# Whether GpSimd or ScalarE makes the upper halves of the first 14 pieces of weights

## The chip, the cores and the metric

One core of a Trainium2 chip runs the whole program. The metric is device time in microseconds (us) from start to end of one launch. The engines are named as the profile names them: PE is TensorE (PEld its weight loads), ACT is ScalarE, DVE is VectorE, POOL is GpSimd and SP the SyncE queue that issues DMAs.

## The reference

Attention with a cut just under each row's maximum, then two feed-forward layers on its output. The attention works on 4 batches of 8 heads with 576 rows of 64 numbers.

```python
scores = scale * q @ k.T                       # per batch and head, 576 x 576
thresh = max(scores, axis=-1) - tau
scores = where(scores >= thresh, scores, -1e9)
attn = exp(scores - max(scores)); attn /= sum(attn) + 1e-09
x = (attn @ v), heads side by side              # 2304 x 512
g = x @ w_gate                                  # d_ff 1536
x = (silu(g) * (x @ w_val)) @ w_out
h = maximum(x @ w_in, 0)                        # d_ff 2048
out = (h * h) @ w_out2                          # 2304 x 512
```

The weights come as float64. The kernel reads their 64-bit words and rebuilds float32 numbers from the bits on the chip, then splits each into a high part that the PE's fast float32 form holds exactly and a low rest, so that three fast products stand for one exact product.

## The kernel before

**Attention.** The work is 144 tiles of 128 rows by 576 columns, nine for each pair of heads and 36 for each batch. Every tile takes the same path. `QK` on the PE makes the scores `s` (two PSUM banks in turn, `s_115` and `s_116` in the orders below). `RED` on DVE takes the row maximum. `CUT` on ACT writes `z`, of which there is one buffer. `EXP` on ACT writes `e` (three buffers, `e_104` to `e_106`) and the row's sum. `RCP` on DVE makes `r`. `NORM` on POOL (line 684) multiplies `e` by `r`. `TR` on the PE transposes `e` into PSUM (five products against `ident`, line 706). `PH` on DVE or ACT copies the transposes to `x_65` (called `x`), and for four of nine tiles `AV` on the PE multiplies by the values (line 762). `QK` of the next tiles runs ahead of `TR`: the tile that is transposed is two or three behind.

**Weights beside it.** While the attention of the first batch runs, the class `Loader` brings in the first 30 pieces of weights, each 128x256 numbers. A piece passes through five steps, written as a generator that yields the engine of its next step. SP loads the 64-bit words (`xF<-in_w`, line 143) into one of three buffers. `few_steps` then copies the top 16 bits of each word into the upper half of a 32-bit word of `head` as a float16 (line 173; two buffers, `head_81` and `head_82`). DVE ors in the middle bits, which gives the float32 piece (line 175, output `xF` or `wf`). ACT copies it to its high part (`wa` or `wx`, line 68), and POOL subtracts to get the low part (`wa<-..,wa`, line 76).

**What sets the order.** In the loop over tiles, `loader.tick(engine)` writes at most one next step of the pieces that wait for that engine, at fixed places of the iteration. A list scheduler then places the instructions with the offsets of the tables `early0` and `early` (`LP` is the tick of POOL, `LA` of ACT, `LD` of DVE). Each engine runs its own list strictly in that order. From tile 36 on, the first feed-forward layer for the finished batch is worked into the attention of the next ones (line 256 is its first product), and after the attention the remaining layers run on the PE alone.

Of the kernel before, what the change touches and what calls it, by code (L numbers as in the profile page):

```python
# [17 lines left out]
AF = mybir.ActivationFunctionType  # L18
# [4 lines left out]
P = 128  # L23
# [59 lines left out]
def attention_moe(tc, qkv, qk0, tau, w1, w2, out, cfg):  # L83
    nc = tc.nc
    ops = Ops(nc)
# [33 lines left out]
    class Loader:  # L119
# [48 lines left out]
        def few_steps(self, raw, fl, whi, wlo, n):  # L168

            head = self.heads[n % len(self.heads)]  # L170
            upper = head.bitcast(F16).rearrange("p (n two) -> p n two", two=2)[:, :, 1]
            yield "A"
            nc.scalar.activation(upper, raw.top, AF.Copy)
            yield "D"
            nc.vector.scalar_tensor_tensor(
                fl.bitcast(I32), raw.mid, 13, head.bitcast(I32), op0=ALU.logical_shift_right, op1=ALU.bitwise_or
            )
            yield "A"
            ops.copy("A", whi, fl)
            yield cfg["wl"][0]  # L180
            ops.sub(cfg["wl"][0], wlo, fl, whi.bitcast(F32))
# [21 lines left out]
    loader = Loader()  # L203
# [253 lines left out]
    heads = {}  # L457
# [388 lines left out]
    def work(i):  # L846

        fstate["credit"] += cfg["rate"]
        if avq:
            at_(AV, avq.pop(0))  # L850
            if fstate["credit"] < cfg["extra"]:
                return
        if fstate["credit"] > 0:
            y = at_(fill_group)
            if y is None:
                fstate["credit"] = 0
            else:
                fstate["credit"] -= y
# [12 lines left out]
    def at_(f, *args, name=None):  # L871
        if name in ("LD", "LA") and 8 <= fstate["i"] < 16:

            with tc.issue_after(st[1]["red" if name == "LD" else "exp"]):
                return f(*args)
        off = cfg["early0" if fstate["i"] < 9 * NPAIR else "early"].get(name or f.__name__, 0)
        if not off:
            return f(*args)
        with tc.high_priority(offset=off):
            return f(*args)  # L880

    for i in range(NTILE + lag + 1):
        mp1.age += 1
        fstate["i"] = i
        t = i - lag - 1
        if i == cfg["three"] + lag:
            mp1.banks = deque(bank[2:])
        if i >= cfg["ldat"] and (i % cfg["lev"] == 0 or i >= 9 * NPAIR):
            at_(loader.start, name="LS")
        at_(loader.tick, "D", name="LD")  # L890
        if i < NTILE:
            at_(RED, i)
            at_(CUT, i)
        if 0 <= t < NTILE:
            at_(PH, t)
            at_(NEG, t)
        if i < NTILE:
            at_(EXP, i)
        at_(loader.tick, "D", name="LD")
        at_(loader.tick, "A", name="LA")  # L900
        at_(mp1.flush, "D", name="FD")
        if 0 <= t < NTILE:
            at_(PL, t)
            if tiles[t][2] in PARTS:
                avq.append(t)
        if 0 <= i - 1 < NTILE:
            at_(RCP, i - 1)
            at_(NORM, i - 1)
        at_(loader.tick, "D", name="LD")
        at_(mp1.flush, "A", name="FA")  # L910
        if i + 1 < NTILE:
            at_(QK, i + 1)
        work(i)
        if 0 <= i - lag < NTILE:
            at_(TR, i - lag)
        at_(mp1.flush, "P", name="FP")
        at_(loader.tick, "P", name="LP")
        at_(loader.tick, "A", name="LA")
        if i < NTILE:
            b, p, k = tiles[i]  # L920
            ha = b * H + 2 * p
            pr = i // 9
            if pr == 0:
                for _ in range((0, 1, 2)[k] if k < 3 else 0):
                    next(first)()
            elif k < 2:
                at_(next, steps, name="PS")
            if pr + 1 < B * NPAIR and k >= 2:
                if k == 2:
                    steps = pair_steps(pr + 1)  # L930
                at_(next, steps, name="PS")
        at_(loader.tick, "D", name="LD")
# [652 lines left out]
def pack(inputs):  # L1585
# [51 lines left out]
    "zs": 1,  # L1637
    "wl": "PD",
    "live": (3, 2),
    "fill": 6,  # L1640
    "om": "D",
    "early0": {
# [19 lines left out]
def program(arrays):  # L1662
    import concourse.bacc as bacc

    nc = bacc.Bacc("TRN2", target_bir_lowering=False, num_devices=1, dynamic_dma_scratch_size=512)
    args = [nc.dram_tensor(n, a.shape, mybir.dt.from_np(a.dtype), kind="ExternalInput").ap() for n, a in arrays]
    out = nc.dram_tensor("out_0_dram", (NT, DM), F32, kind="ExternalOutput").ap()
    with tile.TileContext(nc) as tc:
        attention_moe(tc, *args, out, CFG)
    return nc  # L1670
# [9 lines left out]
```

## Time and profile before

| | |
|---|---|
| median of three runs | 1140.37 us (1140.35 to 1140.4) |
| the profiled execution, whole | 1141.48 us |
| its span, first to last instruction | 1139.7 us |
| busy in the span: PE, DVE, ACT, POOL | 1110.3, 847.6, 678.5, 241.2 us |
| granted clock of the PE | 0.998 |

Busy time is the time in which an engine runs an instruction. An engine that waits for another shows as idle, and the profile names what ended the wait. Ends of the PE's products are modelled, so a busy PE can still hold short waits. 1.8 us of the profiled execution lie outside its span.

### The profile page before, as it was taken

The page shows a single profiled execution, that of the slowest core. Times are in us where ns is not written, and L with a number is a line of the kernel's source. Part 1 is how long each engine was busy: PE and PEld are TensorE (multiplying, and loading weights), DVE is VectorE, ACT ScalarE, POOL GpSimd, SP SyncE. Part 2 cuts the span into 40 slices and gives each one's busy share as a digit, 9 for nine tenths or more (in the row PEclk, how much of TensorE's full clock was granted, in tenths as well). Part 3 has the DMA queues.
Part 4 walks back from the last instruction along what each step waited for, and adds up shares of the span by engine and source line. Part 5 has one row for each costly group of instructions (what it writes and reads, how often), then busy time and mean ns, then how long its engine had stood idle before and what let it go on. Part 6 is the DMA issues. An engine that isn't in the chain of part 4 may idle for free.

```text
span 1139.7 us, 19554 instructions
## 1 busy us (share of the span) xinstructions
PE 1110.3 (97%) x6572; PEld 1010.2 (89%) x6572; DVE 847.6 (74%) x2088; ACT 678.5 (60%) x1594; POOL 241.2 (21%) x365
## 2 busy tenths in 40 slices
PE   7988999999999999999999999989999999999998
PEld 6777999899999999998888888889898998899997
DVE  7887887877787864889985888687658677866554
ACT  7888888988888873554432444345556455543221
POOL 6667655545464521000000000000000000000000
PEclk9999999999999999999999999999999999999999
DMA  7766433344343300332210234355355445443542
GB/s 211 221 190 178 105 96 96 98 110 110 91 100 96 96 1 28 93 93 84 84 56 11 72 141 152 108 175 195 144 207 176 176 158 194 153 159 123 193 174 77
DMA packets 55827, 143.15 MB, mean 126 GB/s; under 512 B 7600, under 2 KB 8880, under 8 KB 55728
## 3 DMA queue, kind: packets, MB, share of 16 engines
q1 hardware_dynamic: 55584, 141.92, 40.4%
q8 instruction: 52, 0.85, 0.3%
q14 instruction: 47, 0.39, 0.1%
q10 hardware_dynamic: 144, 0.00, 0.0%
HBM read 93.06 MB, written 22.28 MB: 101 GB/s over the span
## 4 chain that ended last, share of the span: by engine, by line
PE 79%; DVE 6%; ACT 4%; DMA 2%; issue 1%; POOL 0%; POOLq 0%; ACTq 0%; DVEq 0%; SPq 0%
PE mm L256 17%; PE mm L1490 17%; PE mm L1437 13%; PE mm L301 8%; PE bank L256 6%; PE s L648 4%; PE bank L706 4%; PE bank L765 4%; PE bank L301 4%; DMA wr<-in_w_dram 2%; ACT z L666 1%; DVE st__108 L658 1%; ACT e L674 1%; DVE xs_m L76 1%; ACT pt L726 1%
## 5 line engine op out<-in xcount | busy, mean ns | idle before, releaser
L706 PE MATMUL bank<-ident,e 128*128 128x128 f32 (+1 forms) x720 | 150.5, 275 | 9.3 <-ACT x L68 3.3
L684 POOL TENSOR_SCALAR e<-e,r 128x576 f32<-128x576 f32 x144 | 112.7, 783 | 132.5 <-DVE r L679 106.5
L76 DVE TENSOR_TENSOR pt<-bank,pt 128x384 fp32r<-128x384 f32 x216 | 100.5, 486 | 51.2 <-ACT pt L726 49.5
L256 PE MATMUL mm<-xs,wa 128*128 128x512 f32 (+2 forms) x672 | 125.7, 347 | 0.5 <-ACT x L68 0.5
L256 PEld LDWEIGHTS mm<-xs,wa 128*128 128x128 f32 x672 | 109.5, 188 | 15.7 <-ACT x L68 0.7
L666 ACT ACTIVATE z<-s,thr 128x576 f32<-128x576 f32 x144 | 106.7, 741 | 27.3 <-DVE st__108 L658 21.0
L658 DVE TENSOR_SCALAR_CACHE_REDUCE st__108<-s,tau_c 128x576 bf16<-128x576 f32 x144 | 116.9, 812 | 5.1 <-PE s L648 3.3
L256 PE MATMUL bank<-xs_m,wa 128*128 128x288 f32 x576 | 108.5, 321 | 2.5 <-DVE xF L777 0.9
L706 PEld LDWEIGHTS bank<-ident,e 128*128 128x128 f32 (+1 forms) x720 | 91.2, 135 | 17.3 <-issue 4.6
L674 ACT ACTIVATE e<-z 128x577 f32<-128x577 f32 x144 | 99.5, 691 | 1.7
L726 ACT ACTIVATE pt<-bank 128x384 fp32r<-128x384 f32 x216 | 88.4, 437 | 18.6 <-PE bank L706 17.1
L256 PEld LDWEIGHTS bank<-xs_m,wa 128*128 128x128 f32 x576 | 87.0, 188 | 5.5 <-DVE xs_m L76 2.0
L765 PE MATMUL bank<-pt,vs 128*128 128x256 f32 (+1 forms) x480 | 90.5, 318 | 0.4 <-ACT pt L726 0.3
L648 PE MATMUL s<-kh,qs 128*128 128x288 f32 x256 | 77.9, 318 | 7.6 <-DVE qs L534 5.9
L256 PE MATMUL mm<-xs,wb 128*128 128x512 f32 (+1 forms) x360 | 74.9, 368 | 0.0
L1507 DVE TENSOR_TENSOR xF<-xF,mm 128x512 f32<-128x512 f32 x54 | 37.0, 685 | 50.9 <-PE mm L1490 50.9
L765 PEld LDWEIGHTS bank<-pt,vs 128*128 128x128 f32 x480 | 71.9, 189 | 1.6 <-ACT pt L726 0.7
L648 PE MATMUL s<-kl,qs 128*128 128x288 f32 x256 | 73.1, 300 | 0.0
L256 PEld LDWEIGHTS mm<-xs,wb 128*128 128x128 f32 x360 | 62.9, 189 | 11.3
L68 ACT ACTIVATE wb<-wf 128x256 fp32r<-128x256 f32 x82 | 34.0, 414 | 65.2 <-DVE wf L1094 39.6
L1091 ACT ACTIVATE wf<-wr 128x256 f32<-128x256 f32 x64 | 27.6, 433 | 73.5 <-DMA wr<-in_w_dram 55.1
L1490 PE MATMUL mm<-wb,wx 128*128 128x512 f32 x270 | 67.1, 389 | 0.0
(154 smaller groups left out, 2550.8 us busy)
## 6 DMA issues: line engine op xcount, KB each, us to landing
wr<-in_w_dram SPq DMA_DIRECT2D x106, 256.0 KB, 2.9
raw<-in_qkv_dram SPq DMA_DIRECT2D x15, 896.0 KB, 4.6
kh<-land SPq DMA_DIRECT2D x60, 144.0 KB, 2.6
kl<-raw SPq DMA_DIRECT2D x60, 144.0 KB, 2.8
xF<-in_w_dram SPq DMA_DIRECT2D x30, 256.0 KB, 3.4
right<-kept1T SPq DMA_DIRECT2D x8, 768.0 KB, 5.3
right<-kept0T SPq DMA_DIRECT2D x7, 768.0 KB, 5.4
right<-kept SPq DMA_DIRECT2D x6, 768.0 KB, 4.4
```

Of the source, the lines that this page charges most:

```text
L76: e.tensor_tensor(out, a, b, op=ALU.subtract)
L256: mm(pt[:, :n], w[:, a, col + c * P : col + (c + 1) * P], xs[:, b, c, :], start=(i == 0), stop=(i == len(TERMS) - 1),)
L301: mm(pt[:, :n], w[:, a, 2 * DM + m * P : 2 * DM + (m + 1) * P], u[:, b, :], start=(k == 0), stop=(k == last),)
L648: mm(sp[:, cols], l, r[:, cols], start=(n_ == 0), stop=(n_ == len(pairs) - 1),)
L658: red = nc.vector.tensor_scalar(st_, st[t]["s"][:, :S], scalar1=tau_c, scalar2=None, op0=ALU.subtract, op1=ALU.max, accum_out=th)
L666: nc.scalar.activation(z[:, :S], st[t]["s"][:, :S], AF.Prelu, bias=st[t]["thr"], scale=-1.0, alpha=1 / SLOPE)
L674: ex = nc.scalar.activation(e, st[t]["z"], AF.Exp, scale=-SLOPE, accum_out=sum_)
L684: nc.gpsimd.tensor_scalar(e, e, scalar1=r, scalar2=1.0, op0=ALU.mult, op1=ALU.mult)
L706: mm(dst[:n, j], e[:, c0 : c0 + n], ident, is_transpose=True, start=(j == 0), stop=(j == 1),)
L765: mm(o[:, :n], hd["vs"][:, SLOT[k % 5], :], pt[:, k, lo : lo + n], start=(k == 0), stop=(k == 9))
L1437: mm(bank[:, :BK], w[:, a, c * P : (c + 1) * P], t[:, b, c, :], start=(n == 0 and x in ("11", "12", "S1")), stop=(n == 5), skip_group_chec ...
L1490: mm(pt, u[:, b, s * P : (s + 1) * P], w[a], start=(half == 0 and j == 0 and i == 0), stop=(half == 1 and j == 1 and i == 2),)
```

## The change

The generator's first step for a piece now yields POOL for pieces 1 to 14 and ACT for the rest, and the copy goes through the helper that POOL's other copies use (a multiplication by 1 twice, line 72 in the profile). POOL's tick stands twice in an iteration, so that two of its steps can be written there.

```diff
@@ -169,8 +169,9 @@
             head = self.heads[n % len(self.heads)]
             upper = head.bitcast(F16).rearrange("p (n two) -> p n two", two=2)[:, :, 1]
-            yield "A"
-            nc.scalar.activation(upper, raw.top, AF.Copy)
+            eng = "P" if n <= cfg["heads"] else "A"
+            yield eng
+            ops.copy(eng, upper, raw.top)
             yield "D"
@@ -914,7 +915,8 @@
         at_(mp1.flush, "P", name="FP")
-        at_(loader.tick, "P", name="LP")
+        for _ in range(2):
+            at_(loader.tick, "P", name="LP")
         at_(loader.tick, "A", name="LA")
@@ -1637,6 +1639,7 @@
     "live": (3, 2),
+    "heads": 14,
     "fill": 6,
```

Behind the first changed line, line numbers are one higher in the new kernel (two from the tick on, three behind the table's new row). The new order differs at three places that matter.

POOL at its first work on scores, before. `qt` are two small copies for tile 4, `e_104`, `e_105` and `e_106` the `NORM` of tiles 0, 1 and 2, `kl_187` the low part of the second head's keys.

```order
L548 TENSOR_SCALAR qs_185<-raw_182,qscale 128x576
L72 TENSOR_SCALAR qt_124<-qs_144 128x64
L72 TENSOR_SCALAR qt_125<-qs_185 128x64
L684 TENSOR_SCALAR e_104<-e_104,r_175 128x576
L76 TENSOR_TENSOR kl_187<-raw_182,kh_186 128x288 x2
L684 TENSOR_SCALAR e_105<-e_105,r_196 128x576
L684 TENSOR_SCALAR e_106<-e_106,r_222 128x576
L76 TENSOR_TENSOR raw_212<-raw_212,land_214 128x288 x2
L684 TENSOR_SCALAR e_104<-e_104,r_246 128x576
```

POOL at the same place now:

```order
L549 TENSOR_SCALAR qs_185<-raw_182,qscale 128x576
L72 TENSOR_SCALAR head_82<-xF 128x256
L72 TENSOR_SCALAR head_81<-xF 128x256
L72 TENSOR_SCALAR qt_124<-qs_144 128x64
L72 TENSOR_SCALAR qt_125<-qs_185 128x64
L685 TENSOR_SCALAR e_104<-e_104,r_175 128x576
L72 TENSOR_SCALAR head_82<-xF 128x256
L685 TENSOR_SCALAR e_105<-e_105,r_196 128x576
L76 TENSOR_TENSOR kl_187<-raw_182,kh_186 128x288 x2
L76 TENSOR_TENSOR wa<-xF,wa 128x256
L72 TENSOR_SCALAR head_81<-xF 128x256
L685 TENSOR_SCALAR e_106<-e_106,r_222 128x576
```

Two heads now stand ahead of the two `qt` and the `NORM` of tile 0, a third ahead of that of tile 1. `kl_187` has moved behind the `NORM` of tile 1.

PE from the last two transposes of tile 0 (`bank_89<-ident,e_104`) on, before. The products into `s_115` are the first four of eight of `QK` of tile 4.

```order
L706 MATMUL bank_89<-ident,e_104 128x128 x2
L648 MATMUL s_115<-kh_145,qt_124 128x288
L648 MATMUL s_115<-kl_146,qt_124 128x288
L648 MATMUL s_115<-kh_186,qt_125 128x288
L648 MATMUL s_115<-kl_187,qt_125 128x288
```

PE at the same place now:

```order
L707 MATMUL bank_89<-ident,e_104 128x128 x2
L707 MATMUL bank_90<-ident,e_105 128x128
L707 MATMUL bank_90<-ident,e_105 64x128
L707 MATMUL bank_90<-ident,e_105 128x128
L649 MATMUL s_115<-kh_145,qt_124 128x288
L649 MATMUL s_115<-kl_146,qt_124 128x288
L649 MATMUL s_115<-kh_186,qt_125 128x288
L649 MATMUL s_115<-kl_187,qt_125 128x288
```

The first three transposes of tile 1 (`e_105`) stood behind all eight products of tile 4 and now stand ahead of them.

ACT from `CUT` of tile 4 (`thr_239`) to `EXP` of tile 6, before:

```order
L666 ACTIVATE z_107<-s_115,thr_239 128x576
L68 ACTIVATE x_65<-bank_90 128x2x128
L674 ACTIVATE e_105,sum_244<-z_107 128x577
L173 ACTIVATE head_81<-xF 128x256
L666 ACTIVATE z_107<-s_116,thr_264 128x576
L68 ACTIVATE wa<-xF 128x256
L674 ACTIVATE e_106,sum_269<-z_107 128x577
L68 ACTIVATE wa<-wf_80 128x256
L666 ACTIVATE z_107<-s_115,thr_285 128x576
L68 ACTIVATE x_65<-bank_88 128x2x128
L674 ACTIVATE e_104,sum_290<-z_107 128x577
```

ACT at the same place now:

```order
L667 ACTIVATE z_107<-s_115,thr_239 128x576
L68 ACTIVATE x_65<-bank_90 128x2x128
L675 ACTIVATE e_105,sum_244<-z_107 128x577
L68 ACTIVATE wa<-wf_80 128x256
L667 ACTIVATE z_107<-s_116,thr_264 128x576
L68 ACTIVATE wa<-xF 128x256
L675 ACTIVATE e_106,sum_269<-z_107 128x577
L68 ACTIVATE wa<-xF 128x256
L667 ACTIVATE z_107<-s_115,thr_285 128x576
L68 ACTIVATE x_65<-bank_88 128x2x128
L675 ACTIVATE e_104,sum_290<-z_107 128x577
```

The head between `EXP` of tile 4 and `CUT` of tile 5 is gone, and copies of the high part (`wa`) take such places earlier. Over `CUT` of tiles 0 to 17 the list of ACT holds 12 heads and 11 high parts before, and no head and 14 high parts now. From tile 19 on it holds heads at the same tiles as before (19, 19, 21, 21, 23, 26 and so on), of pieces two later, and the last two heads, at tile 41, are gone. DVE's list follows: the first two combinations stand ahead of `RED` of tile 3, which also moves behind the two copies of tile 0's transposes; over tiles 0 to 17 DVE has 14 combinations (11 before) and POOL 14 subtractions (11 before). On the PE the order is the same from tile 13 to the end but for some single transposes.

## Rows read from the trace of the kernel before

**Rows 1.** Busy time, instructions, clock and DMA of stretches.

```profile
core 0: us, PE busy (x) PEld busy (x) DVE busy (x) ACT busy (x) POOL busy (x), PEclk, DMA share, GB/s
...
10.00:50.00 40.00, 38.01 (x219) 32.10 (x219) 33.95 (x94) 36.86 (x90) 27.08 (x38) 1.00 0.71 200
50.00:98.00 48.00, 42.14 (x249) 34.80 (x248) 38.23 (x106) 41.24 (x100) 32.12 (x44) 1.00 0.72 196
...
120.00:1139.00 1019.00, 1006.29 (x5956) 921.57 (x5954) 752.13 (x1827) 575.92 (x1348) 163.83 (x244) 1.00 0.38 118
```

**Rows 2.** What the PE waited for, 10 to 60 us (total, times, longest).

```profile
PE bank L706 <- POOL e L684: 1.3, 2, 1.1
PE s L648 <- ACT z L666: 0.5, 2, 0.3
PE bank L762 <- DVE x L70: 0.2, 1, 0.2
```

**Rows 3.** The same, from 60 us on.

```profile
PE bank L706 <- ACT x L68: 3.3, 5, 1.1
```

**Rows 4.** Groups of ACT, 10 to 50 us: busy us, mean ns | idle before.

```profile
L173 ACT ACTIVATE head<-xF 128x256 f16<-128x256 bf16 x12 | 5.8, 495 | 0.0
...
L68 ACT ACTIVATE wa<-xF 128x256 fp32r<-128x256 f32 x7 | 2.9, 419 | 0.0
```

**Rows 5.** Groups of DVE, 10 to 50 us.

```profile
L175 DVE SCALAR_TENSOR_TENSOR xF<-xF,head 128x256 int32<-128x256 int32 x7 | 3.7, 547 | 0.0
...
L175 DVE SCALAR_TENSOR_TENSOR wf<-xF,head 128x256 int32<-128x256 int32 x4 | 2.5, 627 | 0.3 <-ACT head L173 0.3
```

**Rows 6.** Groups of POOL, 10 to 50 us.

```profile
L684 POOL TENSOR_SCALAR e<-e,r 128x576 f32<-128x576 f32 x17 | 13.7, 808 | 7.9 <-DVE r L679 6.9 <-PE bank L762 0.5 <-PE bank L706 0.4
L76 POOL TENSOR_TENSOR wa<-xF,wa 128x256 fp32r<-128x256 f32 x7 | 5.1, 732 | 0.2 <-ACT wa L68 0.2
L76 POOL TENSOR_TENSOR raw<-raw,land 128x288 fp32r<-128x288 f32 x4 | 3.7, 929 | 2.3 <-ACT land L68 2.3
...
L72 POOL TENSOR_SCALAR qt<-qs 128x64 fp32r<-128x64 f32 x5 | 1.4, 280 | 2.3 <-DVE qs L534 1.7 <-DMA qs<-raw 0.6
```

**Rows 7.** The tile head over the span: ns min/median/max.

```profile
L175 DVE SCALAR_TENSOR_TENSOR xF<-xF,head x20: 394/426/933, 13.6 to 116.8; 128x256 int32<-128x256 int32 x20
```

**Rows 8.** The tile xF, 0 to 13 us.

```profile
L143 SPq DMA_DIRECT2D xF<-in_w_dram x3: 327/432/646, 4.5 to 6.6; - x3
...
DMA to landing us min/median/max: 4.8/5.1/5.3
```

**Rows 9.** POOL in order of time, 5 to 13 us: start, us.

```profile
7.35 0.75 POOL L548 TENSOR_SCALAR qs<-raw,qscale 128x576 fp32r<-128x576 f32 x1 [3.12 <-DMA raw<-in_qk_dram]
...
9.97 0.24 POOL L72 TENSOR_SCALAR qt<-qs 128x64 fp32r<-128x64 f32 x1 [1.66 <-DVE qs L534]
10.19 0.75 POOL L684 TENSOR_SCALAR e<-e,r 128x576 f32<-128x576 f32 x1
11.96 1.56 POOL L76 TENSOR_TENSOR kl<-raw,kh 128x288 fp32r<-128x288 f32 x2 [1.02 <-ACT kh L68]
```

**Rows 10.** The PE in order of time, 8 to 16 us.

```profile
11.67 1.27 PE L706 MATMUL bank<-ident,e 128*128 128x128 f32 x5
12.59 0.59 PE L648 MATMUL s<-kh,qt 128*128 128x288 f32 x1
...
14.65 1.39 PE L706 MATMUL bank<-ident,e 128*128 128x128 f32 x8
15.79 0.38 PE L648 MATMUL s<-kh,qs 128*128 128x288 f32 x1
```

**Rows 11.** DVE in order of time, 8 to 20 us.

```profile
11.99 0.82 DVE L658 TENSOR_SCALAR_CACHE_REDUCE st__108<-s,tau_c 128x576 bf16<-128x576 f32 x1 [0.89 <-ACT kh L68]
```

**Rows 12.** Two stretches at the start, columns as in Rows 1.

```profile
10.00:15.00 5.00, 4.69 (x20) 4.33 (x20) 3.62 (x11) 4.83 (x11) 3.54 (x6) 1.00 0.54 217
15.00:20.00 5.00, 5.00 (x34) 4.57 (x33) 4.57 (x12) 4.50 (x13) 4.16 (x5) 1.00 0.70 184
```

## Prediction

> **What bounds the kernel now.** I began with the busy time of stretches [rows 1]. From 120 us on the PE is busy 1006.29 of 1019 us, so there every microsecond by which the attention of the first batch ends earlier is passed on, and nothing else of this change counts. The pieces 1 to 14 lie in the stretch from 10 to 50 us. There ACT is busy 36.86 of 40 us, DVE 33.95, POOL 27.08, and the PE 38.01. ACT looks like the bound by its share against DVE and POOL, but the PE is busier still. So the second view was the list of what the PE waited for: from 10 to 60 us three kinds of wait of together 2.0 us (1.3 for `NORM` on POOL, 0.5 for `CUT` on ACT, 0.2 for a copy on DVE) [rows 2]. That fits 40 less 38.01. The reader is to see that the PE runs its list nearly without a gap in the stretch in which the change takes work from ACT. The longer waits, such as 3.3 us for copies on ACT, come after 60 us [rows 3], where ACT keeps its heads.
>
> **What is taken from ACT.** Over tiles 0 to 17 ACT loses 12 heads of 0.495 us, 5.9 us, and gains three more copies of the high part of 0.419 us, because the pieces come along sooner [rows 4]: 36.86 - 5.9 + 1.3 = 32.2 us. This could shorten the stretch by 4.7 us if ACT alone set its pace. What the PE can give back is less: its waits, 2.0 us at most. Of these I count the two for `CUT` (0.5) and the one for the copy (0.2) whole, since a head less in ACT's queue brings both `CUT` and the sum for `r` sooner. Of the 1.3 us for `NORM`, 1.1 are one wait [rows 2]; the low parts of the keys (`raw<-raw,land`), which can stand ahead of a `NORM` on POOL, waited 2.3 us in all for ACT's copy `land` [rows 6]. A freer ACT makes that copy sooner, but not before its data have landed, so I take 0.9 of the 1.3. Together **1.6 us are given back**; the ends are 0 and 2.0.
>
> **What POOL pays.** The trace has no copy on POOL from 16-bit words to 16-bit words. The nearest rows are a one-input copy of 64 elements at 0.280 us and a one-input multiplication of 576 at 0.808 [rows 6]. On the line between them 256 elements take 0.280 + 192 x (0.808 - 0.280) / 512 = 0.48 us. From below I bound it by 0.28, since four times the elements of that copy cost no less, and from above by 0.93, the mean of the dearest subtraction with two inputs (288 elements). I take 0.48, because this operation has one input like the two rows on the line. Fourteen heads are 6.7 us, three more subtractions of 0.732 us are 2.2 us, and POOL comes to 27.08 + 6.7 + 2.2 = 36.0 of 40 us. It hides these in the time in which it waited for `r` before a `NORM`, 6.9 us in the stretch [rows 6]. The cover is thin: at 0.77 us for a head POOL would be full (27.08 + 2.2 + 14 x 0.77 = 40).
>
> **What the moved order costs at the start.** This is the term that is on the path for sure if the pieces land late. POOL's list now has two heads ahead of the `NORM` of tile 0. The loads of pieces 1 to 3 were issued from 4.5 to 6.6 us and took 4.8 to 5.3 us [rows 8]: the first is there at about 9.6 us, the second at about 10.6. POOL, free from 8.1 us, therefore stands still, makes the heads until 11.1, then the two `qt` (0.28 each), and starts the `NORM` at 11.65 instead of 10.19 [rows 9]. It ends at 12.4; the transposes of tile 0 on the PE, which began at 11.67, begin 0.75 us later. They took 0.92 us, until 12.59 [rows 10], so now until 13.3. A third head and the `NORM` of tile 1 end at 12.4 + 0.48 + 0.75 = 13.65. For that the PE waits, since three transposes of tile 1 now stand ahead of `QK` of tile 4; with 0.14 us each (1.14 us for eight, 14.65 to 15.79) that product starts at 14.05 instead of 12.59, and ends at 16.1 after its 2.06 us. The low keys `kl` behind that `NORM` are ready at 13.65 + 1.56 = 15.2, just before the last product needs them. Five transposes are left, 0.7 us, so the PE reaches the next `QK` at 16.8 instead of 15.79 [rows 10]. **The start loses 1.0 us.** On DVE the same shows: `RED` of tile 3, at 11.99 us before [rows 11], now stands behind two copies that need tile 0's transposes, some 2 us later; ACT had other work in between. The loss is 0 if the scheduler's places are filled by waits that POOL had anyway. From above: the PE ran 20 instructions in 4.69 busy us from 10 to 15 us and 34 in 5.00 us from 15 to 20, with the granted clock at 1.00 (2.4 GHz) in both rows [rows 12]. If its quicker pace came 3 us later because it stood idle here, 3 x (1 - 20/34) = 1.2 us more are lost, 2.2 in all.
>
> **What is free.** From tile 19 on the heads that ACT keeps stand at the same tiles, and the PE's order is the same, so from 50 to 98 us (PE 42.14 of 48 busy [rows 1]) I count no gain: that stretch only starts sooner or later as a whole. The two heads fewer at tile 41 fall where the PE is full. The loads come a little earlier and take no more queue time. DVE's three more combinations in the stretch are 3 x 0.56 = 1.7 us (6.2 us for eleven [rows 5]), 35.6 of 40, off the path while the PE is the fuller one.
>
> **The sum.** 1.0 - 1.6 = -0.6 us. For a profiled execution that is 1141.48 - 0.6 = 1140.9 us; the median of the runs shown lies 1.1 us below the profiled execution, so **1139.8 us** for the median. With the ends above the likeliest case goes from -2.0 to +2.2 us, 1138.4 to 1142.6. All of it is within 0.2% (2.3 us), about what a measurement of this kernel can tell from no change.
>
> **Rival 1, faster: ACT was the pace after all.** Ends of products are modelled, PEld is busy only 32.10 of 40 us [rows 1], and so a PE that looks full can hide small stalls behind a late `CUT`. Then the whole 4.7 us come back, less the 1.0 us of the start: -3.7, **1136.7 us**. For it speaks that the removed heads stand directly between `CUT` and `EXP` in ACT's list; against it that only 0.5 us of the PE's waits name ACT. Chance 0.25.
>
> **Rival 2, slower: POOL becomes the bound.** If the copy between 16-bit words costs 0.93 us instead of 0.48, POOL needs 27.08 + 13.0 + 2.2 = 42.3 us in 40, and `NORM`, which stands behind heads in its list, is late in every tile: +2.3. At the start the three heads are 0.9 us longer, 1.9 in place of 1.0. Together +4.2, **1144.6 us**. It decides from 0.77 us a head. Nothing in the trace shows such a price for one input. Chance 0.10.
>
> **Rival 3, slower: DVE and POOL block each other.** The combination on DVE reads two tiles in SBUF and takes 0.394 us at the least and 0.933 at the most [rows 7]; in the stretch its mean is 0.547 and 0.627 [rows 5], while POOL works 68% of the time. With POOL at 36.0 of 40, in proportion, the wait above 0.394 grows from 0.18 to 0.24 us, 14 x 0.06 = 0.8 us of DVE, which is free. If instead each of 14 combinations waited out a whole subtraction of 0.732, DVE would need 33.95 - 6.2 + 14 x 1.126 = 43.5 us in 40: +3.5, with the start's 1.0 +4.5, **1144.9 us**. Chance 0.08. The Trainium skill (SBUF — State Buffer, Who interferes with whom) has such a rule: a DVE instruction with two SBUF inputs and a GpSimd instruction that reads SBUF share a port, and the second to start waits for all of the first. By that rule work on POOL is never free to DVE, and the change moves work to the one engine that can slow DVE; the spread of 0.394 to 0.933 us agrees with it, but the means show that most combinations meet little.
>
> **How the numbers follow.** The likeliest case has 0.57, the rivals 0.25, 0.10 and 0.08. Faster by over 0.2% is rival 1, 0.25; within 0.2% the likeliest case, 0.57; slower rivals 2 and 3, 0.18. The range takes in the likeliest case's ends and rival 1, 1136.6 to 1142.6, and leaves 0.18 out.
>
> **What would show it.** Right: heads on POOL at a mean near 0.48 us; from 10 to 50 us ACT near 32, POOL near 36; the first `NORM` at about 11.65 us and `QK` of tile 4 at about 14; waits of the PE from 18 to 60 us well under 2.0 us in all; and from tile 19 on the same gaps at the same tiles, all moved by under 2 us. Wrong: a head above 0.77 us, `NORM` waited for by the PE in most tiles, or tiles 5 to 17 that follow each other clearly faster, so that the gaps of the second half come 3 us or more earlier.

## The result, and the profile after

The changed kernel takes 1146.07 us (median of 6 runs, 1143.58 to 1149.03), the kernel before beside it 1140.38 (1139.53 to 1141.28). The ratio is 1.0052, with a 95% interval of 1.0036 to 1.0067. It is slower by 5.7 us where 0.6 less were forecast. The profiled execution took 1146.45 us with a span of 1144.7, which is 5.0 more than that of before.

The first view is again the busy time of stretches (columns as in [rows 1]), here of the changed kernel.

```profile
10.00:50.00 40.00, 34.37 (x196) 28.48 (x195) 33.38 (x86) 31.31 (x72) 31.52 (x50) 1.00 0.69 197
...
120.00:1139.00 1019.00, 1010.06 (x5982) 925.51 (x5981) 753.96 (x1834) 579.08 (x1355) 164.90 (x246) 1.00 0.37 117
```

From 10 to 50 us ACT fell from 36.86 to 31.31 us and POOL rose from 27.08 to 31.52, as meant. But the PE fell from 38.01 to 34.37, with 196 instructions where there were 219. What it waited for from 10 to 60 us answers to [rows 2]:

```profile
PE bank L707 <- POOL e L685: 4.3, 5, 1.2
PE bank L763 <- DVE x L70: 0.8, 1, 0.8
PE bank L707 <- ACT x L68: 0.4, 1, 0.4
PE s L649 <- ACT z L667: 0.3, 1, 0.3
PE bank L707 <- DVE x L70: 0.2, 1, 0.2
```

2.0 us of waits have become 6.0, and 4.3 of them are for `NORM` on POOL (line 685 now). From 60 us on little changed (3.1 us for ACT's copies, 3.3 in [rows 3]). The PE in order of time shows four of the five places, 3.9 us: one where tile 0 is transposed, and three more in tiles 3 to 5.

```profile
12.63 2.05 PE L707 MATMUL bank<-ident,e 128*128 128x128 f32 x8 [0.81 <-POOL e L685]
14.32 0.59 PE L649 MATMUL s<-kh,qt 128*128 128x288 f32 x1
...
17.62 0.38 PE L649 MATMUL s<-kh,qs 128*128 128x288 f32 x1
...
21.39 0.76 PE L707 MATMUL bank<-ident,e 128*128 128x128 f32 x5 [0.84 <-POOL e L685]
...
23.74 0.77 PE L707 MATMUL bank<-ident,e 128*128 128x128 f32 x5 [1.06 <-POOL e L685]
...
26.22 0.55 PE L707 MATMUL bank<-ident,e 128*128 128x128 f32 x3 [1.19 <-POOL e L685]
```

The head is not what is dear. The tile `head` over the span (ns min/median/max) and the groups of POOL from 10 to 50 us:

```profile
L72 POOL TENSOR_SCALAR head<-xF x14: 476/484/618, 9.6 to 51.3; 128x256 f16<-128x256 bf16 x14
```

```profile
L685 POOL TENSOR_SCALAR e<-e,r 128x576 f32<-128x576 f32 x16 | 12.3, 768 | 6.1 <-DVE r L680 4.8 <-PE bank L707 1.3
L72 POOL TENSOR_SCALAR head<-xF 128x256 f16<-128x256 bf16 x12 | 5.9, 494 | 3.0 <-DMA xF<-in_w_dram 2.7 <-DVE xF L176 0.4
```

POOL still waits 4.8 us for `r` ahead of `NORM`: what is late is the reciprocal on DVE. DVE and ACT in order of time, tiles 3 to 5, after:

```profile
16.60 0.82 DVE L659 TENSOR_SCALAR_CACHE_REDUCE st__108<-s,tau_c 128x576 bf16<-128x576 f32 x1 [0.88 <-PE s L649]
...
17.34 1.39 DVE L601 SCALAR_TENSOR_TENSOR raw<-raw,qscale,land 128x576 fp32r<-128x576 f32 x1
18.66 1.01 DVE L176 SCALAR_TENSOR_TENSOR xF<-xF,head 128x256 int32<-128x256 int32 x1
19.59 0.81 DVE L659 TENSOR_SCALAR_CACHE_REDUCE st__108<-s,tau_c 128x576 bf16<-128x576 f32 x1
...
20.33 0.15 DVE L680 RECIPROCAL r<-sum 128x1 f32<-128x1 f32 x1
...
22.59 0.15 DVE L680 RECIPROCAL r<-sum 128x1 f32<-128x1 f32 x1
...
24.18 0.15 DVE L680 RECIPROCAL r<-sum 128x1 f32<-128x1 f32 x1
```

```profile
17.72 0.19 ACT L675 ACTIVATION_READ_ACCUMULATOR e<-z 128x1 f32 x1
...
19.62 0.19 ACT L675 ACTIVATION_READ_ACCUMULATOR e<-z 128x1 f32 x1
```

POOL beside them, after:

```profile
17.32 2.07 POOL L76 TENSOR_TENSOR raw<-raw,land 128x288 fp32r<-128x288 f32 x2 [0.26 <-ACT land L68]
...
23.86 1.42 POOL L76 TENSOR_TENSOR wa<-xF,wa 128x256 fp32r<-128x256 f32 x2
25.25 0.92 POOL L685 TENSOR_SCALAR e<-e,r 128x576 f32<-128x576 f32 x1
```

And DVE in the kernel before:

```profile
16.11 1.02 DVE L600 SCALAR_TENSOR_TENSOR raw<-raw,qscale,land 128x576 fp32r<-128x576 f32 x1
...
17.52 0.15 DVE L679 RECIPROCAL r<-sum 128x1 f32<-128x1 f32 x1
17.59 0.79 DVE L658 TENSOR_SCALAR_CACHE_REDUCE st__108<-s,tau_c 128x576 bf16<-128x576 f32 x1
...
18.77 0.17 DVE L679 RECIPROCAL r<-sum 128x1 f32<-128x1 f32 x1 [0.38 <-ACT e L674]
```

After, the row's sum of tile 3 is there at 17.91 us (17.72 + 0.19) and its reciprocal comes at 20.33, since a combination of a piece (18.66) and `RED` of tile 5 (19.59) now stand ahead of it in DVE's list. Tile 4 has its sum at 19.81 and its reciprocal at 22.59. Before, the reciprocal of tile 3 (17.52) stood ahead of `RED` of tile 5 (17.59), and that of tile 4 was executed as soon as ACT had the sum.

Two things on POOL have a part in this. The combination at 18.66 us took 1.01 us, where the shortest takes 0.397, and it ran beside the subtractions of 17.32. And the `NORM` of tile 5 (25.25) did not start at its reciprocal (24.18) but behind two more subtractions (23.86), of pieces that had come along sooner.

### The profile page after: what moved, and what is told of

It reads as the page before. It is cut to its first block, busy times and chain, and to the rows that moved or that the text cites. A ratio compares the mean times of both kernels' runs of the same rounds, so it can differ in the third digit from the quotient of the medians.

```text
span 1144.7 us, 19551 instructions
## 1 busy us (share of the span) xinstructions
PE 1112.4 (97%) x6572; PEld 1011.0 (88%) x6572; DVE 851.2 (74%) x2088; ACT 675.2 (59%) x1580; POOL 247.4 (22%) x379
## 4 chain that ended last, share of the span: by engine, by line
PE 77%; DVE 9%; ACT 7%; DMA 3%; issue 2%; POOL 0%; SPq 0%; POOLq 0%; ACTq 0%; DVEq 0%
PE mm L257 17%; PE mm L1492 15%; PE mm L1439 12%; PE mm L302 8%; PE bank L257 6%; PE s L649 5%; PE bank L707 5%; PE bank L766 4%; PE bank L302 4%; DVE st__108 L659 2%; ACT z L667 2%; DMA wr<-in_w_dram 2%; PE bank L763 1%; ACT e L675 1%; DMA xF<-in_w_dram 1%
```

## Experiments

Times are medians in us, with the ratio to the kernel before on the same chip (95% interval). The lag is the start of the n-th of the PE's 6,572 instructions in a trace, less its start in the trace of before, each from the start of its span; n counts from 0. In the trace of before number 20 is at 12.5 us, 40 at 16.3, 80 at 23.4, 220 at 48.8, 550 at 111, 4620 at 746.

| run | median, before | ratio | lag at 20 | 40 | 80 | 220 | 550 | 4620 | span |
|---|---|---|---|---|---|---|---|---|---|
| changed kernel | 1146.07, 1140.38 | 1.0052 [1.0036, 1.0067] | 1.02 | 1.35 | 3.74 | 4.06 | 3.85 | 3.97 | 5.0 |
| e12 the same again | 1145.43, 1140.29 | 1.0044 [1.0032, 1.0056] | 1.39 | 1.76 | 4.12 | 4.43 | 4.01 | 4.14 | 3.6 |
| e4 two ticks alone | 1140.95, 1141.16 | 1.0001 [0.9987, 1.0015] | 0.11 | 0.10 | 0.11 | -0.33 | -1.02 | -0.92 | -1.4 |
| e1 heads 1, 2 on POOL | 1143.35, 1141.16 | 1.0018 [1.0003, 1.0032] | 1.16 | 1.50 | 1.78 | 1.17 | 0.94 | 1.14 | 2.2 |
| e2 heads 3 to 14 | 1142.97, 1141.16 | 1.0019 [1.0007, 1.0031] | 0.14 | 0.48 | 0.92 | 1.72 | 1.18 | 1.22 | 2.0 |
| e3 heads 5 to 14 | 1143.28, 1141.16 | 1.0018 [1.0007, 1.0029] | 0.04 | 0.04 | 0.04 | 1.20 | 0.56 | 0.64 | 1.8 |
| e5 heads 1, 2 later | 1146.78, 1141.18 | 1.0044 [1.0028, 1.0060] | -0.04 | 1.41 | 2.48 | 5.33 | 6.21 | 6.55 | 5.5 |
| e6 RED behind RCP | 1146.61, 1141.18 | 1.0044 [1.0030, 1.0058] | 1.79 | 2.79 | 3.45 | 4.32 | 3.96 | 4.26 | 5.1 |
| e7 no heads 1 to 14 | 1143.22, 1141.18 | 1.0017 [1.0007, 1.0027] | 0.37 | 0.35 | 1.82 | 1.72 | 1.07 | 1.09 | 1.4 |
| e8 14 copies more | 1143.11, 1141.18 | 1.0013 [1.0004, 1.0023] | 2.19 | 1.76 | 2.01 | 1.76 | 1.65 | 1.37 | 1.5 |
| e9 RED ahead of RCP | 1145.26, 1140.29 | 1.0044 [1.0031, 1.0057] | 0.35 | 0.36 | 0.73 | 1.91 | 2.66 | 2.83 | 2.7 |
| e10 e7 with e6 | 1145.88, 1140.29 | 1.0045 [1.0031, 1.0059] | 0.03 | 0.53 | 1.66 | 2.46 | 2.49 | 2.95 | 2.3 |
| e11 heads from 15 on | 1146.36, 1140.29 | 1.0045 [1.0032, 1.0058] | 0.15 | 0.15 | 0.16 | -0.16 | 4.48 | 4.64 | 5.6 |
| e13 pinned, 14 heads | 1142.55, 1141.19 | 1.0015 [1.0004, 1.0026] | 0.98 | 1.15 | 0.34 | 0.67 | 0.49 | 0.49 | 1.1 |
| e14 pinned, 3 to 14 | 1143.38, 1141.19 | 1.0018 [1.0009, 1.0027] | 0.01 | 0.35 | 0.78 | 1.26 | 2.70 | 2.96 | 3.2 |
| e15 pinned, no heads | 1142.70, 1141.19 | 1.0017 [1.0007, 1.0028] | 0.34 | 0.96 | 0.12 | 0.18 | 0.17 | 0.49 | 1.2 |

e4 has the lists of before, so its row shows what one trace is worth: in the columns up to 80 the lag is 0.11 us at most, later ones differ by up to 1 us without any cause in the code. So the columns up to 80 carry the argument. The second trace of the changed kernel bears this out:

> The changed kernel once more, word for word. A second trace of it shows what of its 5.0 us repeats: if the start depends on when the first loads land, product 20 lies anywhere from 0.8 to 2 us behind before; the loss made between products 40 and 80 (tiles 3 to 8) is 2.0 to 2.6 us again if it comes from the order of the lists, and the medians again differ by 5 to 6 us.

It lost 1.39 us up to number 20 (1.02 in the first trace) and 2.36 between 40 and 80 (2.39). Two separate losses, both of which repeat.

**Which heads.** In the changed kernel, the number in the table (e1), or the condition in two ways (e2 and e3):

```diff
-    "heads": 14,
+    "heads": 2,
...
-            eng = "P" if n <= cfg["heads"] else "A"
+            eng = "P" if 2 < n <= cfg["heads"] else "A"
+            eng = "P" if 4 < n <= cfg["heads"] else "A"
```

> Only pieces 1 and 2 are made by GpSimd; pieces 3 on stay with ScalarE. Theory A (the loss comes from the start: two heads that wait for their loads stand ahead of the NORM of tile 0, and from there the reciprocals of tiles 3 to 7 stand one RED later on VectorE): nearly the whole loss is here, 3.5 to 5.5 us slower than before, the same waits of the PE for NORM between 10 and 27 us (about 4 us). Theory B (the loss comes from GpSimd's load and from VectorE and GpSimd blocking each other in the stretch with 14 heads): 2 of 14 parts of it, 0.5 to 1 us slower.

> Pieces 3 to 14 are made by GpSimd, pieces 1 and 2 by ScalarE as before; twelve heads on GpSimd. Theory A: the start has the old order, so the time is that of before within 1 us, and the PE waits for NORM no longer than before (1.3 us from 10 to 60 us). Theory B: 12 of 14 parts of the loss, 3 to 5 us slower, with waits for NORM spread over tiles 3 to 17.

> Pieces 5 to 14 are made by GpSimd. Theory A: the time of before within 1 us. Theory B: 10 of 14 parts, 2.5 to 4 us slower. If ScalarE's relief is worth anything beside a harmless start, this or the run with pieces 3 to 14 is 0.5 to 2 us faster than before.

The heads 1 and 2 alone make the loss of the start (1.50 at number 40) and nothing lasting after it. e2 loses 0.92 us by number 80. Of e3's ten heads the first starts on POOL at 24.98 us, behind number 80, so its 0.04 there says nothing of them; by number 220 its lag is 1.20, and no gain shows anywhere. The medians are 2.2, 1.8 and 2.1 us above before, closer together than the early lags, and neither theory forecast that: A had 3.5 to 5.5 us for e1 and under 1 for the others, B 0.5 to 1 for e1 and 2.5 to 5 for the others.

**The second tick of POOL**, put into the kernel before:

```diff
-        at_(loader.tick, "P", name="LP")
+        for _ in range(2):
+            at_(loader.tick, "P", name="LP")
```

> The kernel before with GpSimd's tick written twice, heads on ScalarE. No GpSimd step finds a second piece waiting in the same iteration, and the order of the engines is unchanged. Both theories: no change, within 0.5 us of before; it also shows how far runs of one program spread here.

The lists are those of before and the time is the same.

**The start.** In the changed kernel the heads of pieces 1 and 2 are held back behind `NORM` of tile 1:

```diff
-            ops.copy(eng, upper, raw.top)
+            with tc.issue_after(st[1]["norm"]) if n <= 2 else nullcontext():
+                ops.copy(eng, upper, raw.top)
...
```

> All 14 heads on GpSimd, but those of pieces 1 and 2 are issued behind the NORM of tile 1. VectorE's list then has RED of tile 3 and the reciprocals of tiles 3 to 7 where they stood before. Theory A (start and late reciprocals make all of the loss): within 0.5 us of before. Theory C (the start, the late reciprocals and GpSimd's load each take a part): about 2 us slower, as with pieces 3 to 14 alone.

The loss up to number 20 is gone (-0.04), but the heads come back as a lump behind `NORM` of tile 1 and 1.41 us are lost by number 40. The time is 5.6 us above before, where 0.5 or 2 were expected. At 40 us a combination on DVE waits for the head of a later piece on POOL, and with it all that stands behind it. The PE and DVE of this kernel in order of time:

```profile
43.09 0.70 PE L764 MATMUL bank<-x 128*128 128x256 f32 x2 [2.24 <-DVE x L70]
```

```profile
40.25 0.93 DVE L177 SCALAR_TENSOR_TENSOR xF<-xF,head 128x256 int32<-128x256 int32 x1 [0.82 <-POOL head L72]
41.10 1.34 DVE L602 SCALAR_TENSOR_TENSOR raw<-raw,qscale,land 128x576 fp32r<-128x576 f32 x1
```

The PE stood for 2.24 us behind a copy that DVE could make only after these two. That head (39.72) had itself waited 1.43 us for its load. So one wait was taken away and others came in the lists made anew; that holding back the first two heads caused this one is not shown.

**POOL's load without any change of the lists.** The kernel before, with 14 more copies of the same kind on POOL into a tile that nothing reads:

```diff
             nc.scalar.activation(upper, raw.top, AF.Copy)
+            if n <= 14:
+                ops.copy("P", loader.spare.bitcast(F16).rearrange("p (n two) -> p n two", two=2)[:, :, 1], raw.top)
...
```

> The kernel before, heads on ScalarE, and for each of pieces 1 to 14 one more copy of the same form on GpSimd into a tile that nothing reads; the lists of VectorE and ScalarE are those of before, and three of these copies stand ahead of the NORM of tile 0. If GpSimd's standing still for loads at the start and its load are what costs: 1.5 to 4 us slower. If the loss needs the changed lists of VectorE: within 0.7 us of before.

POOL in order of time at the start:

```profile
10.52 0.48 POOL L72 TENSOR_SCALAR spare<-xF 128x256 f16<-128x256 bf16 x1 [1.60 <-DMA xF<-in_w_dram]
11.69 0.48 POOL L72 TENSOR_SCALAR spare<-xF 128x256 f16<-128x256 bf16 x1 [0.69 <-DMA xF<-in_w_dram]
...
12.99 0.75 POOL L687 TENSOR_SCALAR e<-e,r 128x576 f32<-128x576 f32 x1
```

Here ACT is not relieved and DVE has the list of before, and `NORM` of tile 0 comes at 12.99 us instead of 10.19 [rows 9], because POOL stands still for two loads that it did not wait for before, and makes a third copy (12.36) ahead of it. That is the whole loss: 1.76 at number 40, 2.01 at 80, 1.76 at 220, so no cost of the other copies shows. Its first copy starts 1.0 us later than the first head in the changed kernel (10.52 against 9.55), since its load lands later; with the third copy that is why its start loses more.

**The late reciprocals.** First in the changed kernel `RED` of tiles 5 to 8 behind the reciprocal of the tile two back, as before; then the opposite in the kernel before, with no other edit (the scheduler places the work around it anew).

```diff
...
-            at_(RED, i)
+            with tc.issue_after(st[i - 2]["rcp"]) if 5 <= i <= 8 else nullcontext():
+                at_(RED, i)
```

```diff
             at_(RED, i)
+            if 5 <= i <= 8:
+                with tc.issue_after(st[i]["red"]):
+                    at_(RCP, i - 2)
+                at_(NORM, i - 2)
...
-            at_(RCP, i - 1)
-            at_(NORM, i - 1)
+            if not 3 <= i - 1 <= 6:
+                at_(RCP, i - 1)
+                at_(NORM, i - 1)
```

> The changed kernel, with RED of tiles 5 to 8 issued behind the reciprocal of the tile two back, as the kernel before had it; the two heads at the start stay. If the late reciprocals cause the loss of tiles 5 to 8: 1.5 to 2.5 us less than the changed kernel, about 3.5 us slower than before, and the three waits of the PE for NORM from 20 to 27 us go. If GpSimd's load causes them: as the changed kernel, 5 to 6 us slower, waits unchanged.

> The kernel before, with one thing of the changed kernel alone: on DVE the reciprocals of tiles 3 to 6 stand behind the maximum of the tile two on (of tiles 5 to 8), as they stand in the changed kernel's list. Work, engines of the heads and the start are those of before. If the late reciprocals make the loss of tiles 5 to 8, the products follow 1 to 2 us later from product 80 on, with waits of the PE for the normalisation on POOL in tiles 3 to 6 of together more than 1.5 us, and the time is about 1.5 us above that of before. If they do not matter and the loss came from the combinations and subtractions that stand ahead, the products follow within 0.4 us of before and the time is the same.

In e6 the three waits for `NORM` in tiles 3 to 5 (0.84, 1.06 and 1.19 us) come down to two, of 0.25 and 0.46. It loses 0.66 us between 40 and 80 (2.39 in the changed kernel), but its start lost 1.4 us more: the first head begins 0.93 us later, and the PE comes to its quicker pace later too (last section). The two are not independent, because a PE that comes later waits less for a late reciprocal. At number 80 the lag is 3.45 us for 3.74, and the time is 5.4 us above before, where 3.5 were expected. e9 loses only 0.37 there, and 1.91 by number 220. What the PE waited for in e9 from 10 to 30 us:

```profile
PE bank L706 <- POOL e L684: 1.5, 2, 1.0
PE bank L762 <- DVE x L70: 0.6, 1, 0.6
PE s L648 <- ACT z L666: 0.3, 1, 0.3
```

The waits have the expected name and sum, but by number 80 the lag is 0.73 us where 1 to 2 were expected: late reciprocals by `RED` alone are a part of the loss up to there, not all of it. The median does not bear this out: e9 is 5.0 us above before, as much as the changed kernel on the same chip (5.1 in e12), while its trace, which is of its fastest execution, has a span of 2.7 more.

**The relief alone.** No head copies at all for pieces 1 to 14, in the list that the scheduler then makes, and with the order of e6:

```diff
-            yield "A"
-            nc.scalar.activation(upper, raw.top, AF.Copy)
+            if n > 14:
+                yield "A"
+                nc.scalar.activation(upper, raw.top, AF.Copy)
```

> The kernel before, with the copy of the head left out for pieces 1 to 14 on every engine; the combination then takes what the head's tile holds. ScalarE is relieved as in the change and GpSimd gets nothing. If a freer ScalarE is worth what the prediction took (1.6 us): 1 to 2 us faster than before. If the earlier combinations and subtractions by themselves push the reciprocals and the low keys back on VectorE and GpSimd, as this kernel's lists show for tiles 0 to 7: no gain, 0 to 2 us slower, though it does less work.

> No copy for the heads of pieces 1 to 14 on any engine (that part of the computation is left out: the upper halves of these pieces' weights are not written), and in addition the maximum of tiles 5 to 8 stands behind the reciprocal of the tile two back, as in the list of before. Without this order that kernel lost 1.3 us in tiles 5 to 8 and was 2.0 us slower than before. If the late reciprocals made that loss, it falls to under 0.4 us and the time lies within 1 us of before; if the relief of ACT is worth 1.6 us on the PE's side, as predicted, it shows now and the time falls to 1.5 us below before. If the pieces' other work on DVE and POOL made the loss, 1 us or more of it stays.

This is the sharpest blow to my reasoning: ACT has 12 copies less to make from 10 to 50 us, POOL none more, and the kernel is slower. Between 40 and 80 it lost 1.47 us (e7) and 1.13 (e10). In e10's list two combinations stand ahead of the reciprocal of tile 3. ACT has that tile's sum at 16.91 us, DVE makes the reciprocal at 19.40:

```profile
16.37 1.37 DVE L601 SCALAR_TENSOR_TENSOR raw<-raw,qscale,land 128x576 fp32r<-128x576 f32 x1
17.66 1.35 DVE L176 SCALAR_TENSOR_TENSOR xF<-xF,head 128x256 int32<-128x256 int32 x2
...
19.40 0.15 DVE L680 RECIPROCAL r<-sum 128x1 f32<-128x1 f32 x1
```

So the pieces that come sooner make the reciprocal late too, without `RED`. e10's median is 5.6 us above before, its trace, again of the fastest execution, 2.3.

**DVE's list held.** The combinations of pieces 1 to 7 are pinned behind chosen reciprocals, and `RED` as in e6: e13 in the changed kernel, e14 and e15 in the kernel before. In e14 the first two heads stay on ACT and those of pieces 3 to 14 go to POOL, and DVE's list is word for word that of before up to the reciprocal of tile 12. In e15 there are no head copies for pieces 1 to 14. Their core is the same:

```diff
+    PIN = {1: 1, 2: 4, 3: 6, 4: 6, 5: 9, 6: 10, 7: 11}
...
             for x in self.live:
+                if not self.phase and eng == "D" and x[6] in PIN and "rcp" not in st[PIN[x[6]]]:
+                    continue
...
+            with tc.issue_after(st[PIN[n]]["rcp"]) if n in PIN else nullcontext():
...
```

> The changed kernel with DVE's list of tiles 3 to 12 put back nearly as before: the combinations of pieces 1 to 7 stand behind the reciprocals of tiles 1, 4, 6, 6, 9, 10 and 11, and the maximum of tiles 5 to 8 behind the reciprocal of the tile two back. All 14 heads stay on POOL, two of them ahead of the first normalisation. If the order of the lists made the loss of tiles 3 to 8, the products lag at no. 80 as much as at no. 20 (1 to 2 us, from the loads at the start) and the span is 2 us below that of the changed kernel. If the heads that POOL executes made it, 2 us more are lost between products 40 and 80 again.

> The same order of DVE's list, word for word that of before up to the reciprocal of tile 12, with the heads of pieces 1 and 2 on ACT as before and those of pieces 3 to 14 on POOL. Neither the start nor the order is changed, so the products follow those of before within 0.4 us up to no. 110 if the order was the cause. If ACT's relief by 10 heads up to tile 17 were worth the predicted 1.6 us, the products from no. 110 on would come that much earlier; I now expect no gain, and a time within 1.5 us of before. With the heads on POOL as the cause, 1 us or more is lost by product 110.

> No copy for the heads of pieces 1 to 14 on any engine (that part of the computation is left out), with DVE's list held nearly as before: the relief of ACT alone. If it is worth the predicted 1.6 us, the products lead by 1 us or more from no. 110 to no. 330. If the PE's waits in this stretch do not hang on ACT, they stand within 0.5 us of before and the time is that of before within 1 us.

e13 has all 14 heads on POOL, and its lag falls from 1.15 at number 40 to 0.34 at 80 where that of the changed kernel rises from 1.35 to 3.74. What the PE waited for from 10 to 60 us, and two reciprocals of DVE:

```profile
PE bank L711 <- POOL e L689: 1.2, 3, 0.6
PE bank L767 <- DVE x L70: 1.1, 2, 0.6
PE s L653 <- ACT z L671: 0.3, 1, 0.3
PE bank L711 <- DVE x L70: 0.2, 1, 0.2
```

```profile
17.68 0.16 DVE L684 RECIPROCAL r<-sum 128x1 f32<-128x1 f32 x1 [0.65 <-ACT e L679]
...
19.68 0.16 DVE L684 RECIPROCAL r<-sum 128x1 f32<-128x1 f32 x1 [0.60 <-ACT e L679]
```

The reciprocals of tiles 3 and 4 now wait for ACT's sum and for nothing on DVE. The waits for `NORM` fall from 4.3 to 1.2 us, the time from 5.1 to 5.7 above before to 1.4. POOL's list is another too in e13 (its third head now stands behind the `NORM` of tile 1, at 15.13 us), and so are ACT's and the PE's: the run shows what the order of the lists is worth, not that of DVE's alone. e15 is the relief with the order held, from 10 to 50 us:

```profile
10.00:50.00 40.00, 37.42 (x220) 31.00 (x219) 34.39 (x96) 34.40 (x80) 27.00 (x39) 1.00 0.72 201
```

ACT is busy 34.40 us there instead of 36.86, and the lag is 0.12 us at number 80, 0.18 at 220 and 0.17 at 550. With this order the relief is worth nothing: the median is 1.5 us above before, though the kernel does less work.

e14 did not do all that I expected: its lag is 0.78 us at number 80 where I had allowed 0.4, and its time is 2.2 us above before. POOL in order of time shows why. One head (14.61) stands ahead of `NORM` of tile 2, which comes at 15.04 instead of 14.69, and one (20.59) in front of the steps ahead of `NORM` of tile 5, at 22.63 instead of 21.84.

```profile
14.61 0.49 POOL L72 TENSOR_SCALAR head<-xF 128x256 f16<-128x256 bf16 x1 [0.36 <-DVE r L683]
15.04 0.75 POOL L688 TENSOR_SCALAR e<-e,r 128x576 f32<-128x576 f32 x1
...
20.59 0.48 POOL L72 TENSOR_SCALAR head<-xF 128x256 f16<-128x256 bf16 x1
...
22.63 1.47 POOL L688 TENSOR_SCALAR e<-e,r 128x576 f32<-128x576 f32 x2
```

So with the order held the heads are not quite free on POOL either: about 0.4 us each where one stands ahead of a `NORM`. In e13 the heads stand elsewhere.

**The heads where the PE does wait for ACT.** The heads of the pieces from 15 on go to POOL, the first 14 stay:

```diff
-            eng = "P" if n <= cfg["heads"] else "A"
+            eng = "P" if n > cfg["heads"] else "A"
```

> The heads of pieces 1 to 14 stay on ACT, and those of the pieces from 15 on, which come along from tile 19 on, go to POOL. The start and tiles 0 to 18 are as before, so nothing is lost there. If ACT's load is worth something where the PE waits for ACT's copies (3.3 us in five waits between 60 and 120 us), the time is 1 to 2.5 us below before. If a freed engine there only moves the wait to another engine, the time is the same within 1 us.

Both expectations failed: the time is 6.1 us above before. The stretch from 60 to 120 us, first before, then in e11:

```profile
60.00:120.00 60.00, 52.90 (x334) 45.62 (x333) 48.85 (x131) 52.78 (x130) 40.76 (x57) 1.00 0.63 170
```

```profile
60.00:120.00 60.00, 50.03 (x297) 42.02 (x296) 48.77 (x122) 45.16 (x106) 46.40 (x70) 0.97 0.63 169
```

ACT fell by 7.6 us and the PE did less. The PE's waits for ACT's copies went from 3.3 to 2.9 us, those for copies on DVE from 1.9 to 5.4. A part is the clock, whose mean is 0.97 in the row. No version here beats the kernel before.

## Why the prediction was wrong

- **What bounds the kernel**: right. From number 550 to 4620 the lag of the changed kernel goes from 3.85 to 3.97, so what the first batch loses is passed on.
- **What is taken from ACT and what POOL pays**: a head's price was right (0.494 us on the mean for 0.48), the sums were not. That ACT came to 31.31 us (32.2 forecast) is luck: the stretch now holds 15 `EXP` where it held 17. In e15, with 17 `EXP` and the 12 heads left out, ACT is busy 34.40 us, 2.5 less than before. The sum took 5.9 us of durations from a busy time in which neighbours overlap (before, a head starts at 22.43 for 0.50 us and `CUT` at 22.78). POOL had 31.52 of 40 us, not 36.0; in e13, whose PE executes 215 instructions there (219 before), it had 32.20. Twelve of the 14 heads lie in the stretch.
- **The start**: the right mechanism and nearly the size. `NORM` of tile 0 began at 11.83 us (11.65), `QK` of tile 4 at 14.32 (14.05), the next `QK` at 17.62 (16.8). The loss is 1.35 us at number 40, 1.76 in e12, for 1.0 with bounds of 0 and 2.2. e1 (1.50) and e8 (1.76) show the same kind of loss without the rest of the change. About 0.5 us of it, by an estimate, is what the forecast had only as its bound: the quicker pace of the PE begins 1.16 us later (16.41 for 15.25, last section), and five products start 0.24 instead of 0.13 us apart.
- **"Together 1.6 us are given back"**: this failed, and it alone turns the sign, since 1.0 less nothing is a loss. e15, with DVE's list held nearly as before and no head copies, gives nothing. The waits that I put down to ACT's queue were not ended sooner by a shorter queue. Waits for other engines stand in their place: 1.0 us for copies on DVE in e15 where there were 0.2.
- **"35.6 of 40, off the path while the PE is the fuller one"**: this is the step that took the time out of the range. I counted DVE's combinations by busy time. In the list they stand ahead of reciprocals, together with `RED` of the tile two on, and a reciprocal of 0.16 us holds back `NORM`, the transposes and so the PE. The loss is 2.39 us between 40 and 80, where 0 were forecast. e13 shows that it is the order of the lists and not the heads that POOL executes: with all 14 on POOL and DVE's list held, it is gone. That DVE's list is the one that counts rests on the rows of tiles 3 and 4 above; at tile 5 subtractions on POOL come in. e9 and e10 show that neither `RED` alone (0.37 by number 80) nor the combinations alone (1.13) make all of it. How the two add was not settled.
- **"From tile 19 on the same gaps"**: right, within what one trace can tell (4.06 at 220, 3.97 at 4620).
- **Rival 1** fell with e15 and e7. **Rival 2** fell with the price of a head. **Rival 3** gave nearly the right time (1144.9) for another reason. The combinations into `xF` did rise from 0.547 to 0.675 us on the mean, but e8, with as many more copies on POOL and DVE's old list, lost nothing after the start, and in e6, with all 14 heads on POOL, their mean is 0.559. What is left of it is what runs beside a combination that stands ahead of a reciprocal: the one at 18.66 us took 1.01. With the preparation of keys in front of it, 1.39 us for 1.02 before, up to 1.0 us of the 2.4 by which the reciprocal of tile 3 is late can be this, by an estimate from these rows; no run separates it. The Trainium skill (SBUF — State Buffer, Who interferes with whom) says that a DVE instruction with two SBUF inputs and a GpSimd instruction that reads SBUF contend. The slow combinations agree with it. It does not say so of every DVE instruction, so "never free to DVE" in the prediction goes further than the rule.

Counted in the profiled executions, 1.35 (start) + 2.39 (order) + 0.23 (up to number 4620) + 1.03 (after it) make the 5.0 us. That last term is not the change's: e12 has -0.57 there, and the two traces lie 1.5 us apart by number 4700, behind the pause of the last section. The 5.7 us of the medians hold a further 0.7, since the profiled execution of before lies 1.10 us above its median and that of the changed kernel 0.38.

What stays open is why the variants end 1.4 to 2.2 us above before in the median where their lags are small, and e9 and e10 at 5 and more. A part is the trace that they are measured against. In the kernel before, ACT stood 0.62 us for a load, until 59.79, and the PE 1.13 for a copy behind it, until 61.80; e4, with the same lists, has neither wait (in e13 they are 1.13 and 1.58, in e14 1.59 and 2.04). Against e4's trace the lags at number 550 are 1.58 us for e3, 1.51 for e13 and 1.19 for e15, near their 2.1, 1.4 and 1.5 in the median. But e4's profiled execution lies 0.94 us below its median, so that this is the whole answer is not shown. Nor is it for e9 and e10.

## What to carry to other kernels

When a step goes to another engine and the lists are made anew, look for the smallest instruction that others wait for (here the reciprocal), and compare what stands ahead of it in the list before and after. Busy time says nothing of that. What an engine's relief is worth can be measured before it is moved: leave the work out, with the other lists held. And an engine that runs its list in order should not be given, ahead of work on the path, a step that waits for a load.

## What the hardware showed that I had not expected

The start depends on when the first load of a piece lands, and that varies: POOL's first head began at 9.55 us in the changed kernel, 9.87 in e12 and 10.48 in e6, and `NORM` of tile 0 at 11.83, 12.20 and 12.60.

The granted clock fell in some executions behind a wait of the PE. In e14 the PE waited 2.04 us for a copy on ACT, until 63.68 us, and then:

```profile
60.00:64.00 4.00, 1.96 (x17) 1.70 (x16) 2.22 (x4) 2.59 (x6) 2.42 (x4) 1.00 0.49 154
64.00:68.00 4.00, 4.00 (x15) 3.23 (x12) 2.78 (x9) 3.57 (x9) 2.73 (x5) 0.57 0.93 198
```

A granted clock of 0.57 means that most of the stretch ran at the lower level of 1.2 GHz, with 15 instructions in 4.00 busy us against 25 in 3.60 before. e14's lag rises from 1.09 at number 275 to 3.17 at 330 there, by the wait and the clock together. In e5 the PE waited 2.24 us, until 43.09, and the clock stayed at 1.00 from 44 to 48 us. A pause of the PE near 755 us does the same in every trace but e5's, for a different time. The stretches from 755 to 760 and from 760 to 765 us were granted 0.71 and 0.61 in the changed kernel, 0.76 and 0.90 in e12, 0.66 and 1.00 in before. The changed kernel and e12 have the same lists, and there they come apart: the lags are 3.97 and 4.14 us at number 4620, 4.21 and 2.68 at 4700, and the spans end 1.4 us apart. In e5 the clock stays at 1.000 over the whole span, and its lag falls from 6.55 at 4620 to 4.82 at 4700.

The PE also starts slow. In the kernel before, the products of `QK` start 0.24 us apart up to 14.41 us and 0.13 apart from 16.01; in the changed kernel the change comes between 16.15 and 17.84, in e13 behind 14.44, in e6 behind 16.92. The clock column shows 1.00 there [rows 12], but it shows that wherever a trace has no record of the clock, and the first record begins at 15.25 us in before, 16.41 in the changed kernel, 14.55 in e13 and 18.55 in e6. So the reading of 2.4 GHz for the row from 10 to 15 us in the prediction is not borne out: a spacing of nearly twice 0.13 us looks like the lower level. From number 40 on all these traces have the quicker pace, so the losses between 40 and 80 are not made by it.
